# The first part of a fused attention and Fourier-mixing kernel: its order of steps given as a sequence of picks

## The chip, the cores and the metric

The kernel runs on one core of a Trainium2 chip. The metric is the time of one execution on the device in microseconds (us); the median of several runs counts.

A core has five engines with a queue each, and every queue runs in order: PE (TensorE, matmuls), DVE (VectorE), ACT (ScalarE), POOL (GpSimd) and SP (SyncE, which only issues transfers here). They wait for each other through semaphores. PE writes to PSUM, which has 8 banks of 512 float32 for each of 128 partitions.

## What is computed

Attention with random features for 8 batches of 8 heads, 576 rows of 64, then a Fourier mixing and a two-layer network over rows of 512.

```python
def phi(x):                                  # omega: 128 x 64
    h = einsum('bhsd,md->bhsm', x, omega) - sum(x * x) / 2
    return exp(h - max(h)) / sqrt(128)
q_p, k_p = phi(q / 64 ** 0.25), phi(k / 64 ** 0.25)
kv, z = einsum('bhsm,bhsd->bhmd', k_p, v), sum(k_p, axis=2)
x = (q_p @ kv) / (q_p @ z + 1e-6)            # heads side by side: 8 x 576 x 512
u = x + real(fft(fft(x, axis=1), axis=2))
un = (u - mean(u)) / sqrt(var(u) + 1e-6)
out = u + maximum(un @ w_ch1, 0) @ w_ch2     # 512 x 2048, 2048 x 512
```

q, k, v and omega are float32; the two weights come as 64-bit floats, and the kernel narrows them.

## The kernel before

The kernel has two parts, each planned and written out by a small list scheduler in the kernel's own source (class `Listing`, line 82). A piece of the program is a generator that yields `Step` objects: an engine (or several that could do it, with a planned duration for each), the events it needs, the buffers it takes and gives back, an event that it makes, and a `bias`. After each yield the generator issues the instructions of that step. `Listing.run` (line 134) keeps, for every stream of steps, its next step in the list `todo`. It works out when each could start, by planned durations, free engines, buffers and PSUM banks (`start` and `banks_at`), takes the one whose planned start plus bias is least, marks its resources as used and lets its generator go on. A stream can fork another (`Fork`). The order in which steps are taken is the order of the instructions in each engine's queue; nothing reorders them later. Which PSUM bank a step gets, and which engine does a step that two could do, follows from the same planned times. The durations in the source are planner's figures and are no measurements.

The first part has these streams, in this order at the call (line 1064):

- `first`, `loads`, `loads_v`, `load_tables`, `frames`: omega, and the loads of k and q (two buffers), v (three) and the Fourier tables on SP.
- `plain_norms`: normalised rows of four plain tiles of 128 rows.
- `mixing`: for each of the 8 batches, `mix` adds and subtracts mirrored rows and columns of x ("folds", lines 641 to 667 on DVE, half of them sometimes on POOL), multiplies by cosine and sine tables over the rows (L685, PE), copies the products out (L695, ACT), multiplies by tables over the columns in three row blocks (L712 and L717, PE), and forms u in `residual`: L733 (ACT) copies one bank, L738 and L741 (DVE) form sums and differences from PSUM, L749 and L750 (DVE for one half of the rows, POOL for the other) add them to x. A block's two PSUM banks come free after L733 and after the last L741.
- three streams `pairs(i)`: the 32 pairs of heads (4 for each batch; pair n belongs to batch n // 4), each through `attn`. For a pair: transposes of k and q (L443 on PE, `kq`; L450 on ACT copies them out as kqT), score products in 64x64 quarters of PE (L517; two groups of four row blocks and one of one), negated row maxima (L461, DVE), exponentials (L478, ACT, one instruction for each row block), the product kv of the features with v and a column of ones (L551, PE), its copy (L565 on DVE or L567 on ACT), transposes of the query features (L443 with `e`; L450 copies them as qeT), numerators and denominators (L594 and L602, PE), and the division (L611, L612 and L614, DVE) into x.
- `w2_parts` (L990, DVE or POOL) and `weight_sums`: sums of weight blocks for the second part, stored to DRAM by L1013 and L1015.
- `block_norms(0)`: normalised rows and their sums for the first block of the second part.
- `plain`: the four plain tiles through the network: L897 (hidden products, PE), their copies (L881 on DVE or L883 on ACT), L920 (output products, PE).
- `weights`: 32 pieces of weight loaded by POOL (L407) and narrowed by `narrow`: a copy of the high words (L380 on POOL or L382 on ACT), the mask of the sign (L384, DVE), shift, merge and mask (L386 and L389, DVE; one step), the low words (L391, DVE), and the sum (L393, POOL).

Each PSUM user takes one bank ("bank") or an aligned pair ("duo"): transposes, L685, L897 and L920 one, L517, L551, L594 and L712 two.

The second part (the remaining rows in blocks of 512, by a Strassen-like scheme with L1102 and L1281 on PE) is planned by a second call of `run` with its own streams (line 1388).

Of the kernel before, what the change touches and what calls it, by code (L numbers as in the profile page):

```python
# [40 lines left out]
TURN = 0.1  # L41
WIDTH = {"bank": 1, "duo": 2}
FMAX = float(np.finfo(np.float32).max)


class Step:
# [35 lines left out]
class Listing:  # L82
# [48 lines left out]
        t = begin(eng)  # L131
        return t + (TURN if eng == PE and step.mode != self.mode else 0.0), eng

    def run(self, streams):
        todo = []

        def go_on(item):
            while True:
                step = next(item[1], None)
                if step is None:  # L140
                    return
                if isinstance(step, Fork):
                    go_on([item[0], step.stream, None, item[3], item[4]])
                    continue
                item[2] = step
                todo.append(item)
                return

        for i, g in enumerate(streams):
            go_on([i, g, None, (0.0, 0.0), NONE])  # L150
        while todo:
            best = None
            for item in todo:
                got = self.start(*item[2:])
                if got is None:
                    continue
                key = got[0] + item[2].bias, item[0]
                if best is None or key < best[0]:
                    best = key, got, item
            if best is None:  # L160
                raise RuntimeError(f"every stream waits: {[i[2].after for i in todo]}")
            _, (begin, eng), item = best
            step = item[2]
            step.eng = eng
            end = begin + step.engines[eng]
            self.free[eng] = end
            if eng == PE:
                self.mode = step.mode
            if step.on_port(eng):
                self.free[PORT] = end  # L170
            done = end + step.late + (HOP if eng != NONE else 0.0)
            if step.kb:
                self.moved = max(self.moved, end) + step.kb / RATE
                done = max(done, self.moved + 1.6)
            for name in step.take:
                if name in WIDTH:
                    n = WIDTH[name]
                    i = self.banks_at(n, begin)[0]
                    self.banks[i : i + n] = [math.inf] * n
                    self.got = Banks(tuple(range(i, i + n)))  # L180
                else:
                    self.buffers[name].remove(min(self.buffers[name]))
            for name in step.give:
                if isinstance(name, Banks):
                    for i in name.ids:
                        self.banks[i] = done
                else:
                    self.buffers[name].append(done)
            if step.makes is not None:
                self.made[step.makes] = done  # L190
            item[3], item[4] = (end, done), eng
            todo.remove(item)
            go_on(item)
# [33 lines left out]
def kernel(  # L227
# [64 lines left out]
    mlpp = early.enter_context(tc.tile_pool(name="mlp", bufs=2))  # L292
# [506 lines left out]
    def events_of(tt):  # L799
        return tuple(sorted({ev for t in tt for _, _, _, ev in rows_of(t)}))  # L800
# [57 lines left out]
    def plain():  # L858
        for j in range(NPLAIN):
            if j == NPLAIN - 1:  # L860

                yield Step(NONE, after=(("x", B - 1, NP - 1),))
            yield from plain_of(j)
# [107 lines left out]
    def w2_parts():  # L971
        yield Step(NONE, take=("slab",) * 4, after=("converted",))
        big = [slabs.tile([128, 2, 4, 128], F32, name="big", tag="slab") for _ in range(2)]
        sums = [slabs.tile([128, 2, 4, 128], F32, name="sums", tag="slab") for _ in range(2)]

        def raw(fh, mh):
            def part(f, m):
                f0, m0 = HF * fh + 4 * f, HM * mh + 128 * m
                return w2[:, f0 : f0 + 4, m0 : m0 + 128]

            return part

        def summed(f, m):
            return big[f][:, m]

        def op(o, l, r, **kw):
            step = Step({DVE: 0.7, POOL: 1.35}, port=True, **kw, bias=-0.63)
            yield step
            eng = nc.gpsimd if step.eng == POOL else nc.vector
            eng.tensor_tensor(out=o, in0=l, in1=r, op=ALU.subtract)  # L990

        b11, b12, b21, b22 = raw(0, 0), raw(0, 1), raw(1, 0), raw(1, 1)
        last = ()
        for i, made_of in (
            (1, b11), (2, b21), (3, b22), (5, (b12, b11)), (6, (b22, summed)), (4, (b21, summed)),
            (7, (b22, b12)),
        ):
            part = made_of
            if isinstance(made_of, tuple):
                part = summed  # L1000
                l, r = made_of
                for f in range(2):
                    for m in range(2):
                        yield from op(summed(f, m), l(f, m), r(f, m), after=last)
            c11, c12, c21, c22 = part(0, 0), part(0, 1), part(1, 0), part(1, 1)
            (t1, t2), (t3, t4) = ((t[:, 0], t[:, 1]) for t in sums)
            for o, l, r in ((t1, c12, c11), (t2, c22, t1), (t3, c22, c12), (t4, c21, t2)):
                yield from op(o, l, r, after=last, makes=("w2t", i) if o is t4 else None)
            last = (("w2l", i),)

            yield Step(SP, 2.2, 4.5, after=(("w2t", i),), kb=7 * 256, makes=("w2l", i))
            for n, t in ((0, c11), (1, c21), (4, c22)):
                nc.sync.dma_start(w2l[i][n].rearrange("p (f m) -> p f m", f=4), t)  # L1013
            for n, t in ((2, sums[0]), (5, sums[1])):
                nc.sync.dma_start(  # L1015
                    w2l[i][n : n + 2].rearrange("l p n -> p l n"),
                    t[:].rearrange("p l f m -> p l (f m)"),
                )
        yield Step(NONE, after=last, give=("slab",) * 4)
# [15 lines left out]
    def weight_sums(groups):  # L1035
        yield Step(NONE, after=("converted",))
        for g in groups:
            f = slice(GW * g, GW * (g + 1))
            f2 = slice(F2 + f.start, F2 + f.stop)
            ops = sums_left(  # L1040
                w1[:, 0:D2, f], w1[:, D2:NDC, f], w1[:, 0:D2, f2], w1[:, D2:NDC, f2],
                *(w1s[g][:, i] for i in range(3)),
            )
            for i, (o, l, r, op) in enumerate(ops):
                yield Step(DVE, 0.7, makes=("w1s", g) if i == 3 else None, port=True)
                if g == 0 and i == 2:
                    o = w1s[0][:, 3]
                nc.vector.tensor_tensor(out=o, in0=l, in1=r, op=op)
# [6 lines left out]
    def pairs(start):  # L1055
        for n in range(start, B * NP, NS):
            yield from attn(n)
# [6 lines left out]
    listing.run(  # L1064
        [first(), loads(), loads_v(), load_tables(), frames(), plain_norms(), mixing()]
        + [pairs(i) for i in range(NS)]
        + [w2_parts(), weight_sums((0,)), block_norms(0, mlpp), plain(), weights()]
    )
    early.close()

# [16 lines left out]
    def relu_sum(o, ps, sb):  # L1087
        nc.vector._custom_dve(TENSOR_ADD_SAT, out=o, in0=ps, in1=sb, s0=FMAX, s1=0.0)  # L1088

# [329 lines left out]
```

## Time and profile before

Four runs took 1225.39, 1229.06, 1227.01 and 1226.81 us; the median is 1226.91. The profiled execution is the first of these, 1225.39 us, with a span of 1223.5 us.

| Engine | Busy, us | Share of the span |
| --- | --- | --- |
| PE (matmuls) | 1188.8 | 97% |
| PE weight loads | 1064.8 | 87% |
| DVE | 744.4 | 61% |
| ACT | 459.4 | 38% |
| POOL | 384.9 | 31% |

PE's first L1102, the start of the second part on PE, is at 464.8 us. The granted clock of PE is 0.9 to 1.0 of full speed in every slice. Some groups of instructions of the first part:

| Line | Engine | What | Count | Mean, ns |
| --- | --- | --- | --- | --- |
| L461 | DVE | row maxima, 128x1024 | 64 | 1220 |
| L478 | ACT | exponential, 128x128 | 576 | 396 |
| L614 | DVE | division, 128x640 | 32 | 825 |
| L384 | DVE | mask, 128x512 | 32 | 452 |
| L386, L389, L391 | DVE | conversion, 128x512 | 32 each | 689, 689, 695 |
| L393 | POOL | conversion's sum, 128x512 | 32 | 1396 |
| L749, L750 | DVE | sum into x, 128 rows | 16 each | 602, 875 |

The busy time of a group leaves out idle time in front of it; a mean duration contains the latency of an instruction, so instructions that follow each other closely overlap. A timeline row gives start and duration in us, engine, line, operation, what is written from what, shape and count, and in brackets the idle time before and what ended it. A wait for several semaphores is put down to the one that came last.

### The profile page before, as it was taken

What the parts mean: (1) busy time and instruction counts of PE and PEld (TensorE: products, weight loads), DVE (VectorE), ACT (ScalarE), POOL (GpSimd) and SP (SyncE); (2) the same over time, 40 slices, a digit from 0 to 9 for tenths busy, and PEclk for the clock granted to TensorE, in tenths of its full rate; (3) what the DMA queues carried; (4) which work ended last, traced back from release to release, by engine and by line L of the source; (5) the groups of instructions that cost most, each with busy time, mean ns of one, the idle gap of its engine ahead of it and who ended that gap; (6) DMA issues with size and microseconds to landing.
All of it is one profiled execution on the core that took longest, in us unless ns stands there. A gap on an engine that the chain in (4) does not pass through costs nothing.

```text
span 1223.5 us, 31624 instructions
## 1 busy us (share of the span) xinstructions
PE 1188.8 (97%) x12705; PEld 1064.8 (87%) x12705; DVE 744.4 (61%) x1521; ACT 459.4 (38%) x1433; POOL 384.9 (31%) x451
## 2 busy tenths in 40 slices
PE   6889899999999999999999999999999999999997
PEld 5778878878878687999899899899899899899897
DVE  4889999887677644384384285285276266267255
ACT  6867767666654321222222222222222222222211
POOL 2443444431111013322422422431431431431421
PEclk9999999999999999999999999999999999999999
DMA  9564654636564324195196096186176277268255
GB/s 266 151 209 143 197 174 142 212 104 218 167 198 151 126 91 155 51 305 170 32 306 187 11 306 189 31 286 191 49 254 203 61 238 227 61 209 257 61 170 176
DMA packets 149059, 206.02 MB, mean 168 GB/s; under 512 B 49329, under 2 KB 62897, under 8 KB 148913
## 3 DMA queue, kind: packets, MB, share of 16 engines
q1 hardware_dynamic: 144224, 187.15, 49.3%
q0 software_dynamic: 4608, 16.78, 4.1%
q8 instruction: 101, 1.65, 0.6%
q14 instruction: 46, 0.37, 0.1%
q10 hardware_dynamic: 80, 0.07, 0.0%
HBM read 172.23 MB, written 35.91 MB: 170 GB/s over the span
## 4 chain that ended last, share of the span: by engine, by line
PE 91%; DVE 5%; ACT 2%; DMA 1%; issue 1%; SPq 0%; DVEq 0%; ACTq 0%
PE banks L1102 32%; PE banks L1281 28%; PE banks L920 5%; PE banks L897 4%; PE banks L443 4%; PE banks L517 4%; PE banks L685 4%; PE banks L551 3%; PE banks L594 2%; PE banks L712 2%; DVE nmx L461 2%; ACT e L478 1%; PE banks L836 1%; PE banks L717 1%; DVE raw L389 1%
## 5 line engine op out<-in xcount | busy, mean ns | idle before, releaser
L1088 DVE CUSTOM_DVE_ANT_0 hid<-banks,s 128x256 f32<-128x256 f32 x192 | 79.7, 423 | 254.9 <-PE banks L1102 254.9
L1281 PE MATMUL banks<-wl,sums 128*128 128x128 f32 x1792 | 220.2, 275 | 0.0
L1281 PEld LDWEIGHTS banks<-wl,sums 128*128 128x128 f32 x1792 | 210.5, 192 | 1.0
L478 ACT ACTIVATE e<-banks,nmx 128x128 f32<-128x128 f32 x576 | 160.6, 396 | 35.0 <-DVE nmx L461 34.9
L1116 ACT ACTIVATE s<-banks 128x256 f32<-128x256 f32 x192 | 73.7, 384 | 255.7 <-PE banks L1102 255.7
L1102 PE MATMUL banks<-unT,w 128*128 128x256 f32 x704 | 167.3, 379 | 0.0
L1102 PEld LDWEIGHTS banks<-unT,w 128*128 128x128 f32 x704 | 132.7, 190 | 17.9 <-issue 0.5
L1256 ACT ACTIVATE s<-banks 128x128 f32<-128x128 f32 x168 | 46.7, 278 | 237.3 <-PE banks L1281 176.0
L1102 PE MATMUL banks<-tt,w1s 128*128 128x256 f32 x512 | 126.3, 379 | 0.0
L461 DVE TENSOR_REDUCE nmx<-banks 128x8 f32<-128x1024 f32 (+1 forms) x96 | 88.1, 952 | 40.5 <-PE banks L517 32.5
L1169 POOL TENSOR_TENSOR hs<-hid 128x256 f32<-128x256 f32 x64 | 46.5, 726 | 198.3 <-DVE hid L1088 173.6
L1102 PEld LDWEIGHTS banks<-tt,w1s 128*128 128x128 f32 x512 | 97.3, 190 | 13.2
L1281 PE MATMUL banks<-wl,hid 128*128 128x128 f32 x768 | 98.9, 275 | 0.5 <-DMA wl<-w2l 0.5
L1281 PEld LDWEIGHTS banks<-wl,hid 128*128 128x128 f32 x768 | 94.0, 192 | 1.9 <-DMA wl<-w2l 0.7
L1261 DVE TENSOR_TENSOR part<-banks,s 128x128 f32<-128x128 f32 x168 | 48.7, 290 | 76.0 <-PE banks L1281 74.9
L1169 POOL TENSOR_TENSOR hs<-hid,hs 128x256 f32<-128x256 f32 x64 | 46.4, 726 | 118.4 <-issue 94.3
L517 PE MATMUL banks<-om,kqT 64*64 64x128 f32 x2304 | 77.6, 278 | 4.0 <-ACT kqT L450 2.6
L830 POOL TENSOR_TENSOR rstd<-rstd,mhalf 128x1 f32<-128x1 f32 x36 | 29.8, 828 | 162.1 <-DVE rstd L828 162.1
L1102 PE MATMUL banks<-unT,w1s 128*128 128x256 f32 x320 | 80.6, 379 | 0.0
L517 PEld LDWEIGHTS banks<-om,kqT 64*64 64x64 f32 x2304 | 64.6, 136 | 15.6 <-issue 5.0
L1281 PE MATMUL banks<-wl,hs 128*128 128x128 f32 x576 | 74.9, 275 | 0.4 <-DVE part L1261 0.4
L393 POOL TENSOR_TENSOR w<-w,raw 128x512 f32<-128x512 f32 x32 | 44.6, 1396 | 93.2 <-DVE raw L391 79.8
(113 smaller groups left out, 1994.2 us busy)
## 6 DMA issues: line engine op xcount, KB each, us to landing
wl<-w2l SPq DMA_DIRECT2D x392, 256.0 KB, 3.8
raw<-in_moe_w_ch_dram POOLq DMA_DIRECT2D x32, 512.0 KB, 5.1
kq<-in_k_dram SPq DMA_DIRECT2D x32, 288.0 KB, 4.0
kq<-in_q_dram SPq DMA_DIRECT2D x32, 288.0 KB, 3.8
vd<-in_v_dram SPq DMA_DIRECT2D x32, 288.0 KB, 3.8
out_dram<-ur SPq DMA_DIRECT2D x68, 128.0 KB, 2.3
u<-us SPq DMA_DIRECT2D x32, 256.0 KB, 4.1
ur<-us SPq DMA_DIRECT2D x32, 256.0 KB, 3.6
```

What stands on the lines that cost most here:

```text
L443: nc.tensor.transpose(ps[:, (j - j0) * 128 : (j - j0 + 1) * 128], src(j), ident[:])
L461: nc.vector.tensor_reduce(nmx[:, :, 0:num], pps[:, :, 0 : MF * num].rearrange("p b (c m) -> p b c m", m=MF), axis=AX.X, op=ALU.max, negate ...
L478: nc.scalar.activation(out=e[:, c + (i if num == 1 else 0), :], in_=pps[:, i, MF * c : MF * c + MF], func=AF.Exp, bias=nmx[:, i, c : c + 1],)
L517: nc.tensor.matmul(pps[cols, c, MF * m : MF * m + MF], lhsT=kqT[rows, j, cols], rhs=om2[rows, :],)
L685: nc.tensor.matmul(yp[:, 0:NK], lhsT=fold[:, c, n, :], rhs=tab[:, c, :], start=(c == 0), stop=(c == NC3 - 1),)
L897: nc.tensor.matmul(hp[:, 0:TP], lhsT=w1[:, dc, 128 * fc : 128 * fc + 128], rhs=unTs[key][:, dc, :], start=(dc == 0), stop=(dc == NDC - 1),)
L920: nc.tensor.matmul(yp[:, 0:DM], lhsT=hs[fc][:, 128 * i : 128 * i + 128], rhs=w2[:, fc, :], start=(fc == 0), stop=(fc == NFC - 1),)
L1088: nc.vector._custom_dve(TENSOR_ADD_SAT, out=o, in0=ps, in1=sb, s0=FMAX, s1=0.0)
L1102: nc.tensor.matmul(ps[:, 0:HT], lhsT=left(dc), rhs=right(dc), start=start and dc == 0, stop=(dc == D2 - 1), skip_group_check=True,)
L1116: nc.scalar.activation(out=s[:], in_=ps[:, 0:HT], func=AF.Copy)
L1169: nc.gpsimd.tensor_tensor(out=o, in0=l, in1=r, op=op)
L1281: nc.tensor.matmul(ps[:, 0:128], lhsT=left[:, f], rhs=wls[j, i, n][:, f], start=start and f == 0, stop=(f == 3), skip_group_check=True,)
```

## The change

`run` takes a second argument, a string of picks. For each step taken it reads one character, a number in base 36, and takes the stream at that place of `todo`; it looks at no other stream, and the planned time and the bias of the steps then don't decide. Where the string has ended, or where none is given, the choice is made as before. The planned start of the step taken is still worked out, and with it the bank, the buffer and the engine that it gets. The first part gets the string `PICKS`; the call of the second part is not edited. Steps, buffers, planned durations and biases in the source are the same.

```diff
+PICKS = (
+    "00e2ede0ebed3dedebfcdcddfeede3fdfhbi8cdefdebfdgafaggec9hddk0kiij2jejgj7lfffffhcdfffdfcggjehegfi7gjbl"
...
+    "1112032232202111100"
+)
...
-    def run(self, streams):
+    def run(self, streams, picks=None):
         todo = []
+        picks = iter(picks or ())
...
         while todo:
+            pick = next(picks, None)
             best = None
-            for item in todo:
+            for item in todo if pick is None else [todo[int(pick, 36)]]:
                 got = self.start(*item[2:])
...
-        + [w2_parts(), weight_sums((0,)), block_norms(0, mlpp), plain(), weights()]
+        + [w2_parts(), weight_sums((0,)), block_norms(0, mlpp), plain(), weights()],
+        PICKS,
     )
```

More of the change, by code (lines that the diff above doesn't have):

```diff
@@ L43 @@
 FMAX = float(np.finfo(np.float32).max)
+PICKS = (
+    "00e2ede0ebed3dedebfcdcddfeede3fdfhbi8cdefdebfdgafaggec9hddk0kiij2jejgj7lfffffhcdfffdfcggjehegfi7gjbl"
+    "hbhkjgkkdihfhi7hci7bfiadgkhhjce9didbhhb7gggbfihbbf97acbhbeghefaie8bc7chhhcgfc7cedddh9dd1ccdfif8eggih"
+    "f6g8ejihichdihidfkhfhgjckgigh6eihggiddebd6dcg9eei7cfhei6ddfgihhj78gmkmiidaggjfigdmlg6khhjcj6agghifgg"
+    "kh6afejekjkjfigji6j8hjjjiilcj9iegcigdhllkmldjmkkf9j80lca5m7bdai6gfikjaljkika6lhjggic9feikeejhgjij5d7"
+    "ldjeafedkdeikjje5g5ielfafej6egkicg8dffgikghjijiee7eeifaaeefhefehdeh7iffd6hb7eeidiedhggiijbkj35fjkjhk"
+    "kfgfhkk3h795g4e4i6khchlijigkjji4hlfjfd8lfhlg4mi64bfgjjedjgibk6ijj5cgcijhicgi6lii9fi9lf6ggdijf6bgd8fe"
+    "icddchifajihj9fgihgjgi6jbhi6degcbg48ffgfh6ii5kjigihf7jgf9ejggafji7gf7egdfh6ficd6dbhfeeh5addfh5be5bff"
+    "c48gai8hg9ageefcj5j7gh6haeeghhjikiehi5mg6lghhl5jjhagd5nglkmlccnjldj9llj45lkjjaemh6gbmlf8f7hgekef6hke"
+    "87cldljj8bkhihbhhdc6ffgadkdf7ad5kdbgjhhig6lgcel5mdjedilaidedejihgjegi5ggjhcf5dgc5c775kccdh489j8ddgff"
+    "h8cbdgiejkkechjhkkki5gj7kgjjjjfjjjh4i7dhhjjfi4k4h4kjchehg6ihk975g5bfejcehg3dgmggiej6m55bf9igig5h66gg"
+    "jjjfiieifh8ege5kdihdlhiheief9k5fimhmcio8hgk7fge5jhgdeifagbgbjeeekhgclgigh7ge8fgefddfaci4icdffhgfid8f"
+    "gjffhgihd6gc6cjeelgf3af8hbiccgchgfebg5c9d6ehdfcfeeagghffbhc6f9egchggh6aeehfeekjccbdfafdf50h0gcgabgea"
+    "7fcdcfabg6be8bd4c9dcdcdbcebe6bcgb6cefbacadfeaca7dcdcdchdf9abca66f8dcbd8b98c8aa9c8dd2eabcc87a7b758697"
+    "a27277ba9688848aa89a99992b98aa9a287a888729d8a993ba8ac9788aede65bdaacb69ba8ba659b54387a986aaa9baccade"
+    "ad9b7bfcecffffde79fe9e6h9bgc3gc3be1eac26e7ebeddbdfeefegd6cdfed2ddf3dadeb3e3cc9dc6c5dbbdcab7b3c72b79b"
+    "acbb8abbb679a6a9bb9ab49c7b38a93caa998888888888899888686981458778888888888888841933648786583b59691776"
+    "a7c67267761bb4bcb6cc9a679a8aaba3f94df49cbaa675793a9aa88778388a88a93995aa39b94a4954585536126424112222"
+    "3333533555523346545266421330442216087635433437704543770334535754155544556455155414437756241426224444"
+    "1112032232202111100"
+)
 class Step:
```

## The prediction

> **What bounds the kernel now.** I read the busy time by stretch first, then PE's waits, then the timelines of PE and DVE around each wait. The stretches are the start, the rest of the first part up to 200 us, the first part after that, and the second part (columns: stretch, its length, busy time and instructions of PE, weight loads, DVE, ACT, POOL, granted clock, DMA share, GB/s).
>
> ```profile
> 0.00:25.00 25.00, 16.52 (x398) 14.34 (x402) 7.56 (x12) 15.36 (x49) 7.69 (x17) 1.00 0.94 275
> 25.00:200.00 175.00, 156.66 (x3359) 135.98 (x3353) 157.11 (x308) 130.34 (x418) 72.20 (x68) 0.99 0.58 172
> 200.00:465.00 265.00, 264.59 (x3931) 211.02 (x3924) 189.85 (x399) 142.72 (x462) 61.35 (x58) 1.00 0.49 154
> 465.00:1223.50 758.50, 750.99 (x5041) 703.48 (x5039) 389.84 (x802) 170.94 (x507) 243.64 (x309) 1.00 0.54 169
> ```
>
> PE is the bound from 200 us on: it is idle for 0.4 us there up to the end of the first part at 465 us. Before 200 us PE and DVE are about equally loaded (156.7 and 157.1 of 175 us) and wait for each other. That is the only stretch of the first part with time to win. PE's waits before 200 us and after it (us in total, times, longest) say for what:
>
> ```profile
> PE banks L443 <- ACT e L478: 6.9, 7, 1.9
> PE banks L551 <- ACT e L478: 3.1, 4, 1.5
> PE banks L517 <- ACT kqT L450: 2.6, 4, 0.8
> PE banks L594 <- ACT e L478: 2.0, 1, 2.0
> PE banks L594 <- DVE x L614: 1.2, 1, 1.2
> ```
> ```profile
> PE banks L897 <- ACT e L478: 0.4, 1, 0.4
> ```
>
> Most are one loop: a score product (L517) ends, DVE takes the maxima (L461, 1.22 us), ACT the exponentials (L478, 1.15 us for four), and only then is a PSUM bank free for the next transposes (L443). Whatever DVE does in front of L461 delays it. The places that the change touches, on PE:
>
> ```profile
> 40.30 1.15 PE L594 MATMUL banks<-kv,qeT 128*64 128x65 f32 x32 [1.19 <-DVE x L614]
> 84.18 1.20 PE L443 MATMUL banks<-ident,kq 128*128 128x128 f32 x9 [1.38 <-ACT e L478]
> 171.05 1.28 PE L551 MATMUL banks<-vd,e 64*64 64x65 f32 x72
> 179.74 1.20 PE L443 MATMUL banks<-ident,kq 128*128 128x128 f32 x9 [1.87 <-ACT e L478]
> ```
>
> and on DVE:
>
> ```profile
> 66.95 0.71 DVE L749 TENSOR_TENSOR x<-x,bmp 128x257 f32<-128x257 f32 x1
> 67.58 2.59 DVE L750 TENSOR_TENSOR x<-x,bmp 128x255 f32<-128x255 f32 x1
> 81.25 0.57 DVE L384 TENSOR_SCALAR raw<-raw 128x512 uint32<-128x512 uint32 x1
> 81.74 2.67 DVE L461 TENSOR_REDUCE nmx<-banks 128x8 f32<-128x1024 f32 x3
> 161.20 0.75 DVE L384 TENSOR_SCALAR raw<-raw 128x512 uint32<-128x512 uint32 x2
> 164.38 1.41 DVE L389 TENSOR_SCALAR raw<-w 128x512 uint32<-128x512 uint32 x1
> 171.94 0.42 DVE L749 TENSOR_TENSOR x<-x,bmp 128x257 f32<-128x257 f32 x1
> 172.28 0.95 DVE L750 TENSOR_TENSOR x<-x,bmp 128x255 f32<-128x255 f32 x1
> ```
>
> **What the change is in the built programs.** It adds no work. The picks are as many as the steps of the first part (1819), so they set all of its order, and from the first L1102 on, PE's order in the second part is unchanged. Engines change in a few places: four copies of kv (L565 and L567) go from ACT to DVE, two hidden copies from DVE to ACT, one first step of a conversion from POOL to ACT, one sum of w2 from DVE to POOL. By the rows of each (0.295, 0.29, 0.71 and 1.56, 0.69) DVE has 4x0.295 - 2x0.29 - 0.69 = 0.09 us less; nothing. PE's first 248 of 513 steps stand in the same order but for one exchange, with the same PSUM banks under other numbers but for a few places. Up to 200 us it is thus DVE's order that differs: mostly the mask step of the weight conversion (L384, 0.42 us) by a few places. From PE's step 415 or so the last three pairs of heads come later among the plain tiles' products. No loads change; some stores and loads on SP change places, with PE waiting for none of them (its only waits for a DMA are at the start).
>
> **Part by part**, against the profiled execution's times:
>
> *A, at 40.30.* Pair 1's numerator product (L594) goes ahead of pair 3's last score product; pair 2's then gets the two banks of pair 2's transposes instead of pair 1's numerators, which DVE reads until 40.15. What is last there now is ACT's copy of qeT (38.33 + 1.46 = 39.8), so it starts at 39.85: 0.45 us gained, and PE is on the chain up to the next score product (43.62). DVE's mask is put before pair 1's division, which ends 0.42 us later, at 40.6, and nobody needs that bank before 43. Bounds: 0 and the whole wait, 1.19.
>
> *B, at 81.25.* The mask before L461 goes behind all three L461. They start when the first half of the score product is in: 80.40 + 1.10 (L517's rows of 32 records) and 0.1 of hand-over make 81.6 instead of 81.74: 0.1 gained (bounds 0 and 0.42); then 84.18 comes 0.1 earlier.
>
> *C, near 95 to 99.* A mask moves from 89.5 behind pair 6's division at 94.8, in front of pair 7's (96.57), the fold (L641, 97.88) and the L461 at 99.30, which had 0.19 to spare: 0.42 - 0.19 = 0.2 lost (bounds 0 and 0.42). Masks near 110 and 124 go into gaps of DVE of 0.81 and 1.14 us: they cost nothing in that cover, 0.42 each without it, and take 0.05 off an L461 that waits for PE anyhow.
>
> A to C: -0.45 - 0.1 + 0.2 - 0.05 = -0.4.
>
> *E, 160 to 177, where DVE is saturated.* One of the two masks at 161.20 is gone (done in an earlier gap): 0.33 gained up to the L461 at 166.43. But then DVE does the sum of the first mixing block (L749 and L750) before the second block's L738 and L741, and kv of pair 14 (L551, 171.05) takes the second block's banks instead of those of a division. From 166.43 - 0.4 - 0.33 = 165.70: L461 1.22, masks 0.86, L738/L741 1.17, L749/L750 1.21 (171.94 to 173.15), L738/L741 1.16: 171.3, so L551 starts at 171.4, 0.35 later than now though 0.7 was won before. Then kv's copy (now on DVE) waits for L551's end, 172.9, and ends at 173.2; the other sum 1.2, a division 1.2, a conversion 1.8: L461 at 177.4 instead of 177.24. Sum up to there: +0.15. Bounds of E: -0.33, if that bank comes free in time, and +0.55, as worked out.
>
> *After 177.* The L461 at 177.24 ends the wait at 179.74; DVE's work up to 189 is the same, a mask now standing between two conversions instead of after both. From 200 us PE has nothing to win but 0.4 us. The late pairs leave cover: the cosine products of batch 7 need the fold after pair 29's division. From that product's end on PE: division 1.2, fold 3.4, latency 0.4, so 5.0 us, against 1.5 (mixing) + 5 x 0.9 (hidden) = 6.0 us of PE's work; 1.0 us to spare. The sine products have as much. Nothing is charged; if DVE were slower by two long L389 (0.97 each over the usual 0.43), 0.9 would be lost.
>
> **Sum:** -0.4 up to 100 us, +0.55 in E, nothing after: +0.15 on the profiled execution's 1225.39 (span 1223.5 and 1.9 around it). The median of the runs, 1226.91, lies 1.5 above it; forecast 1227.1. Under 0.2% (2.5 us) either way counts as no change, being about what a measurement of this kernel can tell. Bounds of the parts: lowest -1.19 - 0.42 - 0.05 - 0.33 - 0.4 = -2.4 (1224.5), highest 0.42 + 0.55 + 0.9 = +1.9 (1228.8). This is the likeliest case's own range: 60%.
>
> **Rivals.**
>
> *Faster: fewer of DVE's long instructions.* L389 takes 0.43 us, but 1.4 us where POOL's sum (L393) of the conversion before runs beside it; four of these (35.70, 78.01, 164.38, 183.31) lie on the chain of waits, 0.97 each. If the moved masks shift three of them out of POOL's way, 2.9 goes, and 0.45 by A: 1226.9 - 3.35 = 1223.6. For it: the order near 183 has a mask between the two conversions. Against it: the others stay back to back, and the mask itself then meets POOL (L384 at 179.84 took 1.05). 22%.
>
> *Slower: the two sums in E meet POOL's.* As put now, DVE's L749 and L750 start just as POOL starts its own pair for the same block. Where that happened at 66.95 they took 3.14 us together (to 70.09) instead of 1.21. If both sums of E do, kv of pair 14 waits 1.93 longer, and the L461 after the second sum another 1.93: 0.15 + 3.86 = +4.0, 1230.9. It decides from 2.3 us over; one long sum alone (+2.1 in all) stays under 0.2%. For it: POOL is free then and follows the same release. Against it: of 16 full-height L750 on DVE only two are over 1.0 us. 18%.
> [...]
>
> *It doesn't reach the time.* The same as the forecast, and held in its 60%.
>
> **How the numbers follow.** Likeliest: no change, 1227.1, own range 1224.5 to 1228.8. Faster by over 0.2%: 0.22; within: 0.60; slower: 0.18. The range for 8 in 10 goes on to the other cases' prices, 1223.0 to 1231.0.
>
> **What would show it.** In the new profile L594 of pair 2 starts near 39.9 with no wait for L614; L461 after L614 near 81.6; L551 near 171.4 behind L741, where now it stands behind L614; PE's first L1102 at 464.8 to 465.2, with PE busy all through 200 to 465. The forecast is wrong if L1102 starts over 2.5 us earlier or later; long L389 or L750 rows before 190 us would then say which rival, and idle PE between 380 and 465 that the late pairs lacked cover.

## The result and the profile after

The changed kernel takes 1225.37 us (median of 48 runs, 1222.71 to 1230.71), the kernel before beside it 1227.46 us (74 runs, 1223.70 to 1231.84): ratio 0.9984, 95% interval [0.9978, 0.9989]. It is 2.0 us faster, by 0.16%. The forecast was no change, +0.15 us. The time lies in its range (1223.0 to 1231.0), and in that of the likeliest case (1224.5 to 1228.8), but the interval excludes no change, and the change went the other way from the sum.

All lines of the source up to the second part are 27 higher now, those of the second part 28: L443 is L470, L461 L488, L517 L544, L551 L578, L594 L621, L614 L641, L641 L668, L384 L411, L386 L413, L389 L416, L393 L420, L407 L434, L738 to L750 are L765 to L777, L1102 is L1130.

The profiled execution of the changed kernel took 1225.01 us (span 1223.2). Its busy time by stretch, with the columns of the same view of before:

```profile
0.00:25.00 25.00, 16.85 (x299) 14.64 (x303) 6.44 (x10) 13.84 (x42) 9.22 (x18) 0.93 0.85 249
25.00:200.00 175.00, 158.19 (x3444) 137.51 (x3448) 158.58 (x310) 131.93 (x425) 70.23 (x66) 0.99 0.60 176
200.00:465.00 265.00, 264.36 (x3934) 210.83 (x3927) 190.43 (x402) 142.69 (x461) 60.60 (x58) 1.00 0.49 155
465.00:1223.50 758.50, 750.92 (x5041) 703.43 (x5039) 388.87 (x802) 170.96 (x507) 243.99 (x309) 1.00 0.54 169
```

From 200 us on nothing has moved: PE is idle for 0.6 us up to 465 us (0.4 before). Between 25 and 200 us it is idle for 16.8 us, 1.5 less than before. The first 25 us show a granted clock of 0.93, where before had 1.00. PE's waits between 25 and 200 us (us in total, times, longest):

```profile
PE banks L470 <- ACT e L505: 5.6, 6, 1.9
PE banks L578 <- ACT e L505: 2.9, 3, 1.5
PE banks L621 <- ACT e L505: 2.0, 1, 2.0
PE banks L621 <- ACT qeT L477: 1.2, 2, 1.0
...
PE banks L544 <- DVE x L641: 0.9, 2, 0.6
PE banks L544 <- DVE ht L908: 0.7, 1, 0.7
...
PE banks L578 <- DVE bmp L768: 0.4, 1, 0.4
```

The wait of L594 for the division L614 (1.2) is gone, and that of L551 for "issue" (0.5), which the trace of before had and the forecast did not price. The largest, for the exponentials, are still there. The rows that the forecast named, on PE and then on DVE:

```profile
41.03 1.41 PE L621 MATMUL banks<-kv,qeT 128*64 128x65 f32 x32 [0.25 <-ACT qeT L477]
...
85.53 1.20 PE L470 MATMUL banks<-ident,kq 128*128 128x128 f32 x9 [1.31 <-ACT e L505]
...
172.29 1.28 PE L578 MATMUL banks<-vd,e 64*64 64x65 f32 x72 [0.37 <-DVE bmp L768]
...
465.06 1.03 PE L1130 MATMUL banks<-unT,w 128*128 128x256 f32 x4
```
```profile
83.08 2.69 DVE L488 TENSOR_REDUCE nmx<-banks 128x8 f32<-128x1024 f32 x3 [0.33 <-PE banks L544]
85.68 0.42 DVE L411 TENSOR_SCALAR raw<-raw 128x512 uint32<-128x512 uint32 x1
...
178.00 1.22 DVE L488 TENSOR_REDUCE nmx<-banks 128x8 f32<-128x1024 f32 x1
```

All stand later than forecast (39.9, 81.6, 171.4), and the second part starts on PE at 465.06, 0.2 later than the 464.84 of before. So these two executions show no gain at all, though the medians are 2 us apart. They are not alike, and that had to be understood first.

**What differs between executions of one kernel.** The trace records the clock granted to PE. It is full but for single stretches of 3.41 us, at times two in a row, at half. The profile of before has one in the first part, at 86.1 us; that of after has two, at 16.4 and 74.5 us. Over the 17 traces of this case there are 30 (pairs counted once), all before 190 us, besides one at the end of every execution. Taking the stretch of 3.41 us just ahead of each and adding up PE's busy time in it gives:

```
kernel             half-clock stretch at (us)    PE's busy share in the 3.41 us ahead of it
before              86.1                         0.40
before, again       16.6  43.9  78.1  91.7       0.45  0.45  0.41  0.46
after               16.4  74.5                   0.45  0.42
after, again        73.1  134.5 (6.83 long)      0.41  0.54
all 30                                           0.40 to 0.54
```

The half-clock stretches follow a stretch in which PE was at most about half busy; from 190 to 465 us PE idles for about 1 us in all, and there is none. Where a stretch begins differs between executions (73.1, 74.5 and 78.1 us above), and the same idle time is punished in one and not in the next: the wait of 1.38 us at 84.18 of before had one behind it, at 86.1, the wait of 1.31 at 85.53 of after had none. By the start times on PE one costs 1.0 us at 16 us, 1.6 at 44, 0.3 to 0.6 at 72 to 86, 1.6 at 135 to 140, and two in a row 2.0 to 2.9; the 1.6 at 181 to 185 is regained by 196 us. Within one execution the stretches lie whole multiples of 3.41 us apart: 8, 10 and 4 of them between the four of the repeat of before, 17 between the two of after. The windows ahead of these 30 were not idle: PE worked in them for 0.40 to 0.54 of the time. Not every such window is followed by half clock: counted on from the stretches in steps of 3.413 us, their length in the trace's clock records, 19 other windows after the first 7 us have a share of 0.44 to 0.54, and none came. So a share near a half is shown to be low enough at times; what decides in that range is not shown.

From L1130 (L1102) to the end of the span all 17 traces take 757.8 to 758.7 us. All that differs, between executions and between kernels, lies in the first part.

### The profile page after: what moved, and what is told of

It is laid out like the page before. It is cut to its first block, busy times and chain, and to the rows that moved or that the text cites. A ratio compares the mean times of both kernels' runs of the same rounds, so it can differ in the third digit from the quotient of the medians.

```text
span 1223.2 us, 31614 instructions
## 1 busy us (share of the span) xinstructions
PE 1190.3 (97%) x12705; PEld 1066.4 (87%) x12705; DVE 744.3 (61%) x1522; ACT 459.4 (38%) x1432; POOL 384.0 (31%) x451
## 4 chain that ended last, share of the span: by engine, by line
PE 92%; DVE 4%; ACT 3%; issue 1%; DMA 0%; SPq 0%; DVEq 0%; ACTq 0%
PE banks L1130 32%; PE banks L1309 29%; PE banks L947 5%; PE banks L924 4%; PE banks L544 4%; PE banks L470 4%; PE banks L712 4%; PE banks L578 3%; PE banks L621 2%; ACT e L505 2%; PE banks L739 2%; DVE nmx L488 1%; PE banks L863 1%; PE banks L744 1%; PE banks L629 1%
## 5 line engine op out<-in xcount | busy, mean ns | idle before, releaser
L1130 PE MATMUL banks<-unT,w 128*128 128x256 f32 x704 | 167.3, 379 | 0.0
L1130 PEld LDWEIGHTS banks<-unT,w 128*128 128x128 f32 x704 | 132.7, 190 | 17.9 <-issue 0.5
L1130 PE MATMUL banks<-tt,w1s 128*128 128x256 f32 x512 | 126.3, 379 | 0.0
L488 DVE TENSOR_REDUCE nmx<-banks 128x8 f32<-128x1024 f32 (+1 forms) x96 | 88.3, 953 | 33.9 <-PE banks L544 30.7
L1130 PEld LDWEIGHTS banks<-tt,w1s 128*128 128x128 f32 x512 | 97.2, 190 | 13.3
L544 PE MATMUL banks<-om,kqT 64*64 64x128 f32 x2304 | 78.6, 280 | 4.2 <-ACT kqT L477 2.4
L1130 PE MATMUL banks<-unT,w1s 128*128 128x256 f32 x320 | 80.7, 379 | 0.0
L544 PEld LDWEIGHTS banks<-om,kqT 64*64 64x64 f32 x2304 | 65.3, 137 | 15.5 <-ACT kqT L477 4.1
L420 POOL TENSOR_TENSOR w<-w,raw 128x512 f32<-128x512 f32 x32 | 43.8, 1368 | 100.9 <-DVE raw L418 81.7
```

Source lines behind the costliest of these rows:

```text
L488: nc.vector.tensor_reduce(nmx[:, :, 0:num], pps[:, :, 0 : MF * num].rearrange("p b (c m) -> p b c m", m=MF), axis=AX.X, op=ALU.max, negate ...
L544: nc.tensor.matmul(pps[cols, c, MF * m : MF * m + MF], lhsT=kqT[rows, j, cols], rhs=om2[rows, :],)
L1130: nc.tensor.matmul(ps[:, 0:HT], lhsT=left(dc), rhs=right(dc), start=start and dc == 0, stop=(dc == D2 - 1), skip_group_check=True,)
```

## The experiments

Each kernel ran 11 or 12 times beside the kernel before. A ratio's interval is about ±0.1%, 1.2 us, so a part of 2 us is rarely resolved by it. Two more readings are used. **At equal clock:** over all runs the time rises by about 0.8 us per 0.001 of mean granted clock lost; fitting this one slope and a constant for each kernel leaves a standard error of 0.37 us (0.19 for the changed kernel, 0.12 for before). What an order changes in the clock itself, through its idle time, is left out of that column. **Offsets:** the start of the same step of PE in two traces, subtracted; where nothing differs the offset stays within 0.1 us over tens of us.

| Kernel | Median, us | Ratio to before, 95% | At equal clock, against before, us |
| --- | --- | --- | --- |
| before, again | 1227.46 | 1.0002 [0.9989, 1.0014] | -0.1 |
| the changed kernel | 1225.37 | 0.9984 [0.9978, 0.9989] | -1.8 |
| the changed kernel, again | 1225.95 | 0.9986 [0.9974, 0.9998] | -1.6 |
| new order to 208 us only | 1224.68 | 0.9986 [0.9974, 0.9998] | -1.8 |
| new order from 208 us only | 1227.03 | 0.9996 [0.9983, 1.0009] | -0.6 |
| A alone (0 to 47 us) | 1227.07 | 0.9997 [0.9987, 1.0007] | -1.3 |
| A undone | 1226.36 | 0.9989 [0.9979, 0.9998] | -0.9 |
| masks alone (47 to 142 us) | 1226.48 | 0.9996 [0.9984, 1.0009] | -0.6 |
| masks undone | 1226.92 | 0.9998 [0.9986, 1.0010] | -0.5 |
| masks B and C alone | 1226.40 | 0.9991 [0.9978, 1.0003] | -0.9 |
| mask B undone | 1224.76 | 0.9985 [0.9977, 0.9994] | -2.5 |
| mask C undone | 1224.99 | 0.9977 [0.9963, 0.9992] | -2.0 |
| 142 to 208 us alone | 1228.31 | 1.0000 [0.9990, 1.0011] | +0.2 |
| 142 to 208 us undone | 1226.17 | 0.9986 [0.9974, 0.9997] | -1.1 |
| mask at 183 us alone | 1228.66 | 1.0002 [0.9989, 1.0015] | +0.4 |
| mask at 183 us undone | 1225.54 | 0.9983 [0.9969, 0.9997] | -1.6 |

The hybrids cut both orders where the steps taken so far are the same set (at 192, 323, 391, 592 and 882 steps of 1819) and record the joined order as picks.

**Clock or order.** The two kernels unchanged:

> The kernel before, run as if it were a change, so that every one of its runs carries its mean granted clock. Theory 1 (the new order itself saves about 2 us): ratio to the kernel before 1.000, and at the same granted clock its runs are about 2 us longer than those of the changed kernel (which were 1223.8 us at 0.997 and 1225.7 us at 0.996). Theory 2 (the order saves nothing, the changed kernel meets fewer stretches at half clock): ratio 1.000 too, but at equal clock the two kernels take the same time within 0.5 us, and this kernel's mean clock is lower by about 0.002 (the changed kernel's runs: 0.97 us per 0.001 of clock).

> The changed kernel once more, beside the others on one chip. Theory 1 and theory 2 both: ratio 0.9984. Its profile is a second sample of where the half-clock stretches fall. Theory 1: once each such stretch before the first L1130 is taken off (about half of its 3.41 us where PE is busy), the first L1130 comes 1 to 2 us before the first L1102 of the kernel before; theory 2: within 0.3 us of it.

The mean clock is 0.9961 for the changed kernel and 0.9956 to 0.9957 for the one before, a difference that would be 0.4 us; at equal clock 1.8 us stay. So it is the order, for the most part. With its window at 73 us (0.45 us) and the two at 134.5 (2.9 us) taken off, the repeated changed kernel reaches L1130 at 463.2; the first with its windows at 16.4 and 74.5 (1.0 and 0.5) taken off at 463.6. The kernel before has 464.84 in the trace that the forecast used; with its window at 86.1 (0.56) taken off, 464.3.

**Front or tail.**

```diff
 PICKS
-steps 0 to 1818 of the new order
+steps 0 to 881 new, 882 to 1818 of before        (front)
+steps 0 to 881 of before, 882 to 1818 new        (tail)
```

> The first 882 picks of the changed kernel (to 208 us), then the order of the kernel before. If the gain is made in the first 208 us (A worth 1.1 instead of 0.45, the wait at 193.7 gone, less E): ratio 0.9984 to 0.999, 1.2 to 2.0 us faster. If my forecast's sum holds and the gain is made later: 1.0001 (+0.15 us). If it is the clock alone: 1.000.

> The first 882 steps in the order of the kernel before, the rest (from 208 us, the late pairs moved among the plain products among it) in the changed kernel's order. If the gain is made in the first 208 us: 1.000, since PE idles only 0.4 us from 200 to 465 us and moving its steps cannot take time out. If the gain is made later: 0.9984. If it is the clock alone: the same as the kernel before where the half-clock stretches are as many, whatever the order.

The front has the whole gain; the tail's 0.6 at equal clock is not resolved from 0. The rearranged late pairs are worth nothing that can be seen, and cost nothing either, as forecast.

**Term A.** The new order of PE is this, with nothing else exchanged on PE up to 221 us:

```diff
 PE
-score product, first 32 matmuls (L544); numerators of pair 1 (L621, L629)
+numerators of pair 1 (L621, L629); score product, first 32 matmuls (L544)
 kv of pair 3 (L578), transposes (L470), numerators of pair 2 (L621)
```

> The kernel before with only the first 192 steps (to 47 us) in the new order: pair 1's numerators go ahead of pair 3's last score product, and one mask is moved. Forecast's term A: pair 2's product of numerators starts 0.45 us earlier and the time falls by 0.45 (ratio 0.9996). Theory after the first traces (the product needs only the first of three qeT copies): it starts about 1.1 us earlier, 0.85 us are left at 55 us, and 0.7 to 0.9 at the first L1130 (ratio 0.9993). If everything behind it is decided elsewhere: 1.000 and nothing left at 200 us.

> The changed kernel with its first 192 steps put back into the order of before. Forecast's term A: 0.45 us over the changed kernel (ratio to before 0.9988). Theory after the first traces: 0.85 over it (ratio 0.9991), the wait of about 1.2 us at pair 2's product of numerators is back. If A carries the whole gain: 1.000.

From 29 to 48 us the offset to before falls by 0.89 us in the kernel with A alone (1.80 to 0.91), by 0.76 to 0.92 in seven others with A and by 0.35 in one; with the old order it rises by 0 to 0.94 in six without a half-clock stretch there. The six rise by 0.29 on average, so against the old order as it mostly runs A is worth about 1.1 us. The wait before pair 2's numerators was 1.19 us and is 0.25. The reason is in these rows of the changed kernel on ACT:

```profile
39.71 0.28 ACT L594 ACTIVATE kv<-banks 128x130 f32<-128x130 f32 x1 [0.70 <-PE banks L578]
40.00 1.47 ACT L477 ACTIVATE qeT<-banks 128x128 f32<-128x128 f32 x3
```

The three copies of qeT last until 41.47, but L621 starts at 41.03: its first matmuls need only the first copies, and it waits 0.25 us in all. The forecast had let it wait for the third. So pair 2's numerators come 1.1 us earlier, and what is left at 48 us is 0.85 us, not 0.45. There can be a second price to the old wait: in the repeat of before it was 1.88 us long, PE was 0.45 busy in the stretch with it, and the half-clock stretch at 43.9 behind it cost another 1.6 us (offset 3.37 to 4.97).

**The masks from 47 to 142 us.**

```diff
 DVE, near 81 us (B)
-mask L411, maxima L488 x3, conversion L413
+maxima L488 x3, mask L411, conversion L413
 DVE, 88 to 95 us (C)
-maxima L488, mask L411, differences L765 ... division L641, conversion L413
+maxima L488, differences L765 ... division L641, mask L411, conversion L413
```

> The kernel before with only steps 192 to 592 (47 to 142 us) in the new order: the mask moves of B, C and those near 110 and 124. Forecast: -0.1 + 0.2 - 0.05 = +0.05 us (ratio 1.0000), a loss of 0.2 near 98 us. Rival (the kernel before has a loss of 0.6 to 1.3 us between 93 and 104 us that its profiled execution did not show, because a half-clock stretch lay just ahead of it, and the new order avoids it): ratio 0.9990 to 0.9995, and PE passes from 93 to 104 us in 10.1 us and not in 10.9 or more.

> The changed kernel with only steps 192 to 592 (the mask moves between 47 and 142 us) put back into the order of before. Forecast's terms B, C and the mask near 124: 0.05 us faster than the changed kernel. Theory now (these moves lose 0.24 at 98 us but keep PE's instruction packet ahead of the weight load at 94 us, and keep the fold at 98 us clear of POOL): 0.3 to 1.0 us slower than the changed kernel, ratio to before 0.9988 to 0.9993; in the trace the packet of the chunk begun at 88 to 92 us starts over 1.5 us behind it.

This is the largest part: undone, it takes 1.35 us of the gain at equal clock. Alone it brings 0.6. Where the trace has no half-clock stretch between 48 and 128 us, the offset rises by 0.68 us in the tail kernel, which has the old masks, and falls by 0.61 and 0.67 in two with the new ones; with one stretch near 74 us it rises by 0.37, 1.64 and 1.85 with the old masks, and by -0.06 to 0.12 with the new. With two or more there is no clear difference (0.72 and 2.31 with the old, 1.85 and 2.33 with the new). These offsets are to the trace that the forecast was made from, so that one is the 0: it has the old masks, and passed this part faster than any other trace with them, although its half-clock stretch at 86.1 cost it 0.56 us (eleven other traces gain that much on it between 88 and 91 us). What the old masks cost elsewhere stands on PE in the kernel with the masks undone:

```profile
93.77 0.57 PE L578 MATMUL banks<-vd,e 64*64 64x65 f32 x21
95.21 1.03 PE L578 MATMUL banks<-vd,e 64*64 64x65 f32 x51 [0.88 <-issue]
```

One product of kv, 72 matmuls that depend on nothing among themselves, stops after 20 or 21 of them and goes on 0.88 us later, for "issue", that is, for nothing that the profile shows.

**What "issue" is.** PE's instructions come over DMA too. The page of after lists them:

```profile
q1 hardware_dynamic: 144224, 187.15, 49.3%
q0 software_dynamic: 4608, 16.78, 4.3%
q8 instruction: 101, 1.65, 0.6%
```

There are 101 packets in q8, each of 16 KB (16384 bytes). PE has 25410 matmuls and weight loads and 422 instructions of its sequencer, nearly all for semaphores: 25832 in all, or 256 to a packet, 64 bytes each. The idle times for "issue" inside a product lie at the same few places of that count in different traces, above all 961, 3521 and 7361, which are multiples of 256 apart. So the packet of the next 256 instructions was late. Below are the two places that matter, from the DMA records; times count from the start of the chunk of 256 ahead:

```
                        POOL's load    packet   packet   next chunk   late by
                        issued         starts   done     begins
next chunk from 3521, the kv product at 94 us; 4.59 without delay
before                  -1.76          +1.58    +2.54    +4.59        0
tail                    -1.19          +2.82    +3.79    +5.23        0.64
A alone                 -1.19          +2.50    +3.46    +4.95        0.36
142 to 208 us alone     -1.20          +3.50    +4.47    +5.96        1.37
masks undone            -1.20          +3.43    +4.39    +5.73        1.14
mask B undone           -1.70          +2.58    +3.54    +5.01        0.42
after                   -0.74          +2.45    +3.41    +4.67        0.08
masks B and C alone     -0.65          +0.88    +2.59    +4.59        0
front                   -0.52          +0.59    +1.80    +4.59        0
next chunk from 7361, the kv product at 195 us; 3.76 without delay
before                  -2.11          +2.26    +3.22    +4.54        0.78
142 to 208 us undone    -2.11          +2.10    +3.06    +4.53        0.77
mask at 183 undone      -2.11          +2.21    +3.17    +4.56        0.80
A alone                 -2.11          +1.55    +2.52    +3.79        0.03
mask at 183 alone       -3.53          +0.21    +2.00    +3.76        0
after                   -2.85          +0.60    +1.56    +3.77        0
front                   -3.06          +0.10    +1.42    +3.77        0
```

The next chunk begins 1.3 to 1.5 us after its packet is done, or at PE's own pace if that is later. A packet takes 0.96 or 0.97 us in 12 of these 16 rows and 1.21 to 1.79 in the others, but it starts up to 3.5 us after the chunk ahead is begun, when the 512 KB load of raw that POOL issues (L434) is on the DMA engines: either the packet goes out ahead of that load or it starts when much of the load is through (at its start 47% of the load's bytes had landed in after and 77% in before at 94 us, 99% or more in both at 195 us). These runs show which of the two went first, but not why a packet that comes second waits for up to 3.5 us.

POOL issues that load behind its sum L420, which waits for DVE's conversion, which waits for the mask. So a mask of 0.42 us on DVE decides whether PE gets its instructions in time. One exchange near 183 us tests this alone:

```diff
 DVE
-mask L411 (b), conversion L413 L416 L418 (a), conversion L413 L416 L418 (b)
+conversion L413 L416 L418 (a), mask L411 (b), conversion L413 L416 L418 (b)
```

> The kernel before with one single exchange: near 183 us the mask of one weight conversion goes behind the other conversion's two operations instead of ahead of them, so POOL's sum and the 512 KB weight load that POOL issues behind it come about 0.4 us earlier or more. Fetch theory (PE's idle time in the middle of the kv product at 195 us is a late 16 KB packet of PE's instructions, behind that weight load on the DMA engines): the packet starts less than 1.6 us after its chunk of 256 instructions is begun, where it took 2.0 to 2.3 us in four traces with this order, the idle time (0.25 to 0.51) is gone and 0.5 to 0.75 us are won from 195 us on. Forecast's reading (a mask between two conversions instead of behind both costs nothing, and there is no such packet): 0. The ratio alone (0.9994 or 1.0000) can hardly tell; the start times on PE do.

> The changed kernel with only that exchange undone. Fetch theory: the weight load comes later again, the packet that PE needs at 195 us starts 1.6 us or more behind its chunk and the idle time of 0.25 to 0.75 us in the kv product is back (+0.25 to +0.75 us from there on). Forecast's reading: 0.

The product at 195 us in the kernel before with this one exchange, and in the changed kernel without it:

```profile
197.89 1.28 PE L578 MATMUL banks<-vd,e 64*64 64x65 f32 x72
```
```profile
194.72 0.92 PE L578 MATMUL banks<-vd,e 64*64 64x65 f32 x44
196.16 0.68 PE L578 MATMUL banks<-vd,e 64*64 64x65 f32 x28 [0.52 <-issue]
```

It does what the theory says, in both directions: the stop comes and goes with the mask. So it is in the other traces: with the mask between the conversions the packet is in time in all nine, with the mask ahead of both it is late by 0.5 to 0.8 us in seven of eight (0.03 in the eighth). The time does not follow: neither kernel differs from its parent beyond 0.4 us at equal clock. The offsets say why. In the first of the two a half-clock stretch at 184.8 hides it. In the second the offset is 1.00 at 181 us and 1.03 at 196; in the front kernel, with the exchange, it goes from -1.14 to -0.40 at the score product of 190 us, which waits 0.75 longer for DVE (ht, L908), and then to -1.22 when the stop does not come. With the mask between, the second conversion's L413 takes 1.66 us beside POOL's work instead of 0.67, which gives back part of what the packet wins: 0.07 to 0.09 us are left in three traces without such a stretch and 0.60 to 0.61 in three others, 0.34 on average. That is less than the runs can resolve.

The same for the two masks of B and C, each way:

> The kernel before with only steps 323 to 391 in the new order: the two masks of B and C. Forecast: -0.1 at 82 us, +0.2 at 98 us, so +0.1. Theory after the second set of traces: +0.24 at 98 us, and PE's idle time inside the kv product at 94 us (0.37, 0.41 and 1.11 us in three of five traces with the order of before, none in five with the new one) does not come; on average that is -0.2 to -0.5. If it comes by chance, whatever the masks: it can be in this trace, 0.3 to 1.1 us.

> The changed kernel with only B's mask put back ahead of the three maxima near 81 us. Forecast's term B: +0.1 us. Fetch theory (the mask ahead of its conversion holds POOL's weight load back by some 0.4 us, so that PE's packet goes first): the load is issued more than 0.9 us before the chunk of 256 instructions is begun at 88 to 92 us (0.5 to 0.75 in the changed order), the packet starts more than 2.4 us behind the chunk, and PE idles 0.05 to 1.3 us inside the kv product at 94 us. If B has no part in that: packet and load as in the changed kernel, no idle time there.

> The changed kernel with only C undone: the second mask goes back to its place ahead of the first mixing block's differences. Forecast's term C: 0.2 us faster than the changed kernel (0.24 by the traces since). Rival (the same move is what keeps the instruction packet in time at 94 us): the idle time of 0.3 to 1.1 us in the kv product at 94 us comes back and the time is 0 to 0.9 us longer than the changed kernel's.

C costs 0.23 to 0.25 us between 93 and 99 us in seven of the nine traces that have it, and nothing where it is undone: forecast 0.2. (In the other two the stop at 94 us stands there, with 0.30 and 0.47.) Its rival falls, no idle time at 94 us came back. For B the stop came back (0.42 us, with the load issued 1.70 ahead), but in time this kernel is, if anything, the fastest at equal clock. So B's mask alone is not shown to carry the gain of the masks; which of the moves does is not settled. Of nine traces with B's mask put behind, one has a stop of over 0.2 us at 94 us (0.25); of eight with it ahead, five (0.36 to 1.37).

At the maxima themselves B does more than the forecast's 0.1. With the mask behind, the way from the second half of the score product (82.05 us on PE of before) to the next transposes (84.18) is 0.34 to 0.48 us shorter in five of the nine traces. In the other four the maxima wait for the score product first, for 0.33 us or more, as at 83.08 above, and nothing is won; nor is it in any of the eight with the mask ahead. On average that is -0.2 us. DVE and PE of the front kernel, one of the five (the wait of 0.91 was 1.38):

```profile
81.20 2.89 DVE L488 TENSOR_REDUCE nmx<-banks 128x8 f32<-128x1024 f32 x3
```
```profile
83.66 1.20 PE L470 MATMUL banks<-ident,kq 128*128 128x128 f32 x9 [0.91 <-ACT e L505]
```

**142 to 208 us.**

```diff
 DVE, 166 to 173 us
-differences L765 L768 (1), division, differences (2), sums L776 L777 (1), sums (2)
+differences L765 L768 (1), sums L776 L777 (1), differences (2), division, sums (2)
```

> The kernel before with only steps 592 to 882 (142 to 208 us) in the new order: the sums ahead of the differences at 172 us, kv of pair 14 in other banks, one mask gone at 161 us and one put between conversions near 183 us. Forecast's term E: +0.55 (ratio 1.0004). Theory after the first traces: +0.45 at pair 14's kv, but the idle time in the middle of the kv product at 195 us (0.5 us, with nothing shown that it waits for) and the long sum before it are gone: -0.3 to -0.6 at 208 us (ratio 0.9996). If E and what follows carry the whole gain: 0.9984.

> The changed kernel with only steps 592 to 882 (142 to 208 us) put back. Forecast's term E: 0.55 us faster than the changed kernel. Theory now (the two sums cost 0.67 us each on DVE in the new order and not 1.21, one mask is gone, and the idle time of 0.73 us in the kv product at 195 us is gone): 0.3 to 0.9 us slower than the changed kernel; in the trace the idle time of 0.5 to 0.75 us is back at 195 us.

Undone it costs 0.7 us at equal clock, alone it brings nothing that is seen (+0.2). The kernel with it alone kept the old masks and had the largest stop at 94 us (1.37) in its one trace; whether that hid the gain in its other runs is not shown. The offsets are the same in all nine traces with the new order: -0.27 at 170 us, +0.45 at kv of pair 14, -0.47 up to 176, so -0.3 in all. The forecast had +0.55. DVE and POOL of the changed kernel, and POOL of before, show where it erred:

```profile
170.33 0.41 DVE L776 TENSOR_TENSOR x<-x,bmp 128x257 f32<-128x257 f32 x1
170.66 0.41 DVE L777 TENSOR_TENSOR x<-x,bmp 128x255 f32<-128x255 f32 x1
...
173.85 0.42 DVE L776 TENSOR_TENSOR x<-x,bmp 128x257 f32<-128x257 f32 x1
174.18 0.42 DVE L777 TENSOR_TENSOR x<-x,bmp 128x255 f32<-128x255 f32 x1
```
```profile
170.50 1.16 POOL L776 TENSOR_TENSOR x<-x,bmp 128x257 f32<-128x257 f32 x1 [1.02 <-DVE bmp L768]
171.63 0.63 POOL L777 TENSOR_TENSOR x<-x,bmp 128x255 f32<-128x255 f32 x1
```
```profile
172.12 0.82 POOL L749 TENSOR_TENSOR x<-x,bmp 128x257 f32<-128x257 f32 x1 [1.03 <-DVE bmp L741]
172.91 0.82 POOL L750 TENSOR_TENSOR x<-x,bmp 128x255 f32<-128x255 f32 x1
```

Before, DVE's two sums (171.94 to 174.26) ran beside POOL's pair at 172.12 to 173.73 and took 1.21 and 1.11 us. Now DVE's first pair starts 0.17 ahead of POOL's, takes 0.67 (170.33 to 171.00), and POOL's L776 pays instead, with 1.16 where it took 0.72 at 169.77 us of before, with no sums on DVE beside it; the second pair on DVE meets nobody, and POOL's work there is on no path. Who starts first does not say which of the two pays: before, too, DVE's pair started 0.18 ahead of POOL's (171.94 and 172.12), and there DVE's L750 took 0.95. What decides it is not shown.

## Why the prediction was wrong, point by point

- **What bounds the kernel:** right. From 200 us on PE is busy and nothing came of the rearranged late pairs; the front alone gives 0.9986, as the changed kernel beside it.
- **A, -0.45:** right mechanism, too small. 0.85 us by the offsets, or 1.1 against the mean of the traces with the old order, since the numerators need not wait for the third copy of qeT.
- **B, C and the masks near 110 and 124, +0.05:** this step failed. C is as forecast (0.24 against 0.2), the masks near 110 and 124 move no offset between 104 and 128 us, and B wins 0.2 on average where 0.1 was forecast. But the moves were priced by DVE's time in front of the next maxima alone; undone together they cost 1.35 us at equal clock (standard error 0.4). What they set in motion was left out: POOL's weight load moves, and PE's instruction packet with it. One stop at 94 us is 0.36 to 1.37 us, in five of eight traces with B's mask ahead. The stop accounts for some 0.4 us on average (0.5 against 0.07). With B and C that makes 0.4 of the 0.6 (alone) to 1.35 (undone) us; the rest of this part has no measured owner.
- **E, +0.55:** this step failed by size and sign; it measures -0.3. The gain of the mask gone was right (-0.27 against -0.33), and so was the wait of pair 14's kv for L768. But both sums were priced at 1.21 us from a row in which POOL's pair ran beside DVE's; in the new order the first takes 0.67, 0.54 less, and the second meets nobody either.
- **After 177, 0:** the trace of before did show the wait for "issue" in L551 and the forecast passed over it. It goes (0.8), and about half of that is given back by a conversion that meets POOL: 0.07 to 0.61 us are won, 0.34 on average.
- **The base.** The sum was made on one execution of 1225.39 us. The median of 74 is 1227.46. That execution had neither the stop at 94 us nor a half-clock stretch before 86 us, so it did not hold all of what the new order takes away. Its own time at the first L1102 is 464.84; the kernel with the old front and new tail, its one half-clock stretch (1.56 us) taken off, gets 465.3.
- **Rivals.** Three of the four long L389 are still there in the trace of after (37.53, 79.42 and 165.11 us), so that rival did not make the gain; the sums in E met POOL, but POOL paid. "It doesn't reach the time" fell with the interval.

The time fell into the forecast range, but not by the forecast sum: three of its terms erred, all in the same direction. The terms as measured, A -0.85 to -1.1, masks about -1 (0.6 alone, 1.35 undone), 142 to 208 us -0.4 to -0.9 and the tail 0, make -2.3 to -3.0 us against -2.0 by the ratio and -1.8 at equal clock; the errors of the parts allow it. The traces alone, as means with the new place of each move less means with the old, give A -1.1, B -0.2, the stop at 94 us -0.4, C +0.2, E -0.3 and the exchange at 183 us -0.2, so -2.0. These are means of six to nine traces, and the half-clock stretches are not in them. No version beats the changed kernel beyond doubt: the two with a mask undone lie 0.2 and 0.7 us below it at equal clock, with errors of 0.4.

## What to carry to other kernels

Price a row only after looking at what ran beside it: a duration read beside another engine's work is a price for that neighbourhood (here 1.21 us for two sums beside POOL's pair, and 0.67 for the same two in the new order), and a reorder changes the neighbourhood. A stop inside a run of independent instructions for "issue" is a wait too; count instructions in chunks of what one packet brings (256 here) and look at what the DMA engines carried when the next chunk was wanted. And before a sum is made on one profiled execution, see where that execution stands among the runs: where effects of 1 us come and go, an execution near the fastest does not show what the typical one pays.

## What the runs showed of the hardware

- The clock granted to PE halved for one or two stretches of 3.41 us after a stretch in which PE was 0.40 to 0.54 busy (30 cases, but not after every such stretch); idle time can thus cost twice, 0.3 to 1.6 us more for one stretch and 2.0 to 2.9 for two in a row.
- PE's instructions arrive in packets of 16 KB, 256 instructions each, by DMA like the data (101 packets of 16384 bytes for 25832 instructions). With matmuls of 65 columns a chunk lasts 3.8 to 4.6 us; a packet that started 2.0 to 3.5 us after the chunk ahead was begun stopped PE for up to 1.4 us.
- A DVE operation of 0.42 us, moved behind three others, made such a stop come and go (the mask at 183 us: in time in nine of nine traces, late in seven of eight).
